# Splitting the state recurrence of an S4 layer's channel loop into two alternating vector chains

## The chip, the core and the metric

The kernel runs on one core of a Trainium2 chip. The metric is the device time of one execution in microseconds (us); lower is better. Before the change three runs took 2869.94, 2877.78 and 2879.02 us, so the median is 2877.78 us.

A core has a matrix engine (TensorE, "PE" in the profile, with its weight loads as "PEld"), a vector engine (VectorE, "DVE"), a scalar engine (ScalarE, "ACT"), a general engine (GpSimd, "POOL") and an engine that mostly issues transfers (SyncE, "SP"). Each has its own instruction queue and runs it in order. Engines wait for each other, and an instruction waits for an earlier one of its own engine, through semaphores that finished instructions raise.

## The reference, cut to what matters

The program computes a gated mix of two layers over 2048 tokens of width 576, and all gradients of it. One layer is multi-head attention (32 heads of 18), the other a diagonal state-space layer (S4) with 128 complex states per channel, written in the reference as a long convolution:

```python
def _fwd_reference(A_x, ..., B_Dskip, gate_w):
    x = A_x                                             # (1, 2048, 576)
    g = _sigmoid((x * gate_w).sum(-1, keepdims=True))
    a = _A_ref(x, A_wqkv, A_wo)                         # attention
    b = _B_ref(x, B_A_re, ..., B_Dskip)                 # S4
    return g * a + (1 - g) * b

def _B_ref(u, A_re, A_im, B_re, B_im, C_re, C_im, log_dt, Dskip):
    dt = jnp.exp(log_dt)[:, None]
    logdA = dt * (A_re + 1j * A_im)                     # (576, 128)
    dB = dt * (B_re + 1j * B_im)
    P = jnp.exp(logdA[:, :, None] * l[None, None, :])   # l = 0 .. 2047
    K = jnp.einsum("dn,dnl,dn->dl", Cc, P, dB).real
    ...                                                 # y = causal convolution of u with K, by FFT
    return y + u * Dskip[None, None, :]

def reference(...):
    _out, _vjp = jax.vjp(_f, A_x, ..., gate_w)
    return (_out, *_vjp(grad_out))                      # output and 12 gradients
```

The kernel does the convolution without an FFT. It cuts the 2048 tokens into 16 chunks of 128. Inside a chunk it multiplies by small Toeplitz matrices; from chunk to chunk it carries the 128 complex states of each channel, H(k) = UV(k) + Z * H(k-1), where Z is the state's factor over 128 tokens. The gradient needs the same recurrence once more, on the output gradient in reversed order (the adjoint states, G). Both recurrences use the same Z and do not depend on each other.

## The kernel before

The program has four stages in a row: projections and parameter preparation, the attention forward and backward pass (0.2 to 2.2 ms of the span), the channel loop of the S4 layer (from about 2.2 to 2.7 ms), and a final stage with the weight gradients and the outputs.

**The channel loop.** `for i in range(NBLK)` (line 1182) runs over 18 blocks of `CB` = 32 channels. The 128 states lie on the 128 partitions; channels and chunks lie along the free dimension. The order of the work on each engine is the order of the code (the stage is written under a manual schedule). In iteration `i` it is, for the computing engines:

- `k0(i+1)`, `uv(i+1, 0)`, `turn_e(i+1, 1)`: matrix products on TensorE, evacuated by ScalarE, that prepare the next block. `uv` produces `UV`, the input of the recurrence (bfloat16).
- `scan(i, 0, 15)` (lines 548 to 563): the two recurrences of block `i` on VectorE. The tile `HG` holds 4 rows (real and imaginary part `r`, times forward and adjoint `s`), 15 chunks and 32 channels in float32. A copy (line 553) fills chunk 0, then 14 steps of three instructions follow: a product with the real and the imaginary part of Z together (line 559, 256 elements per partition), the addition of `UV` (line 562, 128 elements) and the addition of the crossed half (line 563, 128 elements). Each of the three reads what the one in front of it wrote.
- `casts(i)` on ScalarE: bfloat16 copies `hR` and `gR` of the states (line 570).
- `rw1(i)` and `rw2(i)` on VectorE (lines 578, 584, 585): the states times parameters, which make `Rw`.
- `t0(i)`, `uv(i+1, 1)`, `ybp(i)`: TensorE products; `ybp` multiplies `Rw` (tile `yp`) and waits for it.
- `pairs1(i)` and `pairs2(i)`: products of states on VectorE (lines 629 and 657, tile `pq`), summed by TensorE into `misc`.
- `turn_e(i+2, 0)`, `m_sum`, `m_fin`, `sums(i)`, `m_part(i+3)`: further preparation on TensorE and ScalarE, and one short pair of instructions on GpSimd.

The loads of later blocks (`E1n`, `xs`, `T0w`, about 1 MB each) are issued by SyncE one to three iterations ahead. VectorE has nothing in the loop but `scan`, `rw1`, `rw2`, `pairs1` and `pairs2` of one block, then the same of the next. The final stage begins when the buffers of the loop come free, and its first weight gradients (`ps_dwq`) follow the last block's TensorE work.

The tile `tz` is a temporary of the recurrence with two buffers. `par` holds, for each block, Z as eight rows of 32 channels: four times the real part, then the imaginary part with the signs of the four rows.

Of the kernel before, what the change touches and what calls it, by code (L numbers as in the profile page):

```python
# [9 lines left out]
A = mybir.AluOpType  # L10
ACT = mybir.ActivationFunctionType
BF = mybir.dt.bfloat16
F32 = mybir.dt.float32
# [4 lines left out]
P = 128  # L18


def build(tc, aps, dbg_aps=None, stages=("s1", "attn", "post", "s4", "final")):
    nc = tc.nc
# [39 lines left out]
    with ExitStack() as gctx:  # L62
# [38 lines left out]
        CB = 32  # L101
# [329 lines left out]
        Q = {}  # L431
# [73 lines left out]
        def blk(b):  # L505
            if b not in BK:
                B_ = BK[b] = dict(E={}, En={})
            return BK[b]
# [39 lines left out]
        def scan(b, k0, k1):  # L548
            B_ = blk(b)
            UVk = B_["UV"][:, :, 0:2 * NB, :].rearrange("p r (s k) c -> p r s k c", s=2)  # L550
            if k0 == 0:
                B_["HG"] = Q["pw"].tile([P, 4, NS, CB], F32, tag="HG", name="HG")
                nc.vector.tensor_copy(B_["HG"][:, :, 0, :].rearrange("p (r s) c -> p r s c", s=2), UVk[:, :, :, 0, :])
                k0 = 1
            HG = B_["HG"]
            ZZ = B_["par"][:, 0:8, :].rearrange("p (m q) c -> p m q c", m=2)
            for k in range(k0, k1):
                tz = Q["pw"].tile([P, 2, 4, CB], F32, tag="tz", bufs=2, name="tz")
                nc.vector.tensor_tensor(tz, HG[:, :, k - 1, :].unsqueeze(1).to_broadcast([P, 2, 4, CB]), ZZ, op=A.mult)  # L559
                t0v = tz[:, 0].rearrange("p (r s) c -> p r s c", s=2)  # L560
                t1v = tz[:, 1].rearrange("p (r s) c -> p r s c", s=2)
                nc.vector.tensor_tensor(t0v, t0v, UVk[:, :, :, k, :], op=A.add)  # L562
                nc.vector.tensor_tensor(HG[:, :, k, :].rearrange("p (r s) c -> p r s c", s=2), t0v, t1v[:, ::-1], op=A.add)  # L563

        def casts(b):
            B_ = blk(b)
            HGv = B_["HG"].rearrange("p (r s) k c -> p r s k c", s=2)
            for nm, s_ in (("hR", 0), ("gR", 1)):
# [5 lines left out]
        def rw1(b):  # L574
            B_ = blk(b)
            for nm, r_, tg in (("wa", 8, "wA"), ("wb", 9, "wB")):
                B_[nm] = Q["pw"].tile([P, 4 * NS, CB], F32, tag=tg, name=nm)
                nc.vector.tensor_tensor(B_[nm], B_["HG"].rearrange("p q k c -> p (q k) c"),
                                        B_["par"][:, r_, :].unsqueeze(1).to_broadcast([P, 4 * NS, CB]), op=A.mult)
# [118 lines left out]
        if "attn" in stages:  # L698
# [5 lines left out]
            with ExitStack() as ctx:  # L704
# [293 lines left out]
                for G in range(NTOT + OFF + 24):  # L998
# [4 lines left out]
                    if G < NTOT:  # L1003
                        u, s = divmod(G, NST)
# [28 lines left out]
                    elif 0 <= m_ < NTOT // 8:  # L1033
# [14 lines left out]
                        else:  # L1048
                            p = 2 * kq + (slot == 4)
# [41 lines left out]
                    for (kind, g, b, i, j, ps) in rows:  # L1091
# [9 lines left out]
                        else:  # L1101
# [6 lines left out]
                            if U["dsn", i] == nj:  # L1108
                                p = i // 2
# [15 lines left out]
        if "s4" in stages:  # L1125
# [8 lines left out]
            with ExitStack() as ctx:  # L1134
                pc = ctx.enter_context(tc.tile_pool(name="s4l", reuse_waits="tile", bufs=1))
                pw = Q["pw"] = Q["en", 2] = ctx.enter_context(tc.tile_pool(name="s4lw", reuse_waits="tile", bufs=1))
# [45 lines left out]
                for i in range(NBLK):  # L1182
# [17 lines left out]
                    if cur:  # L1200
                        scan(i, 0, 15)
                        casts(i)
                        rw1(i)
                        rw2(i)
                        t0(i, 0)
                        t0(i, 1)
# [33 lines left out]
        if "final" in stages and "s4" in stages:  # L1240
# [14 lines left out]
            with ExitStack() as ctx:  # L1255
# [18 lines left out]
                with ExitStack() as actx:  # L1274
# [87 lines left out]
                    s_ = [SS[:, q, :] for q in range(6)]  # L1362
# [173 lines left out]
```

## Time and profile before

| what | value |
| --- | --- |
| runs | 2869.94, 2877.78, 2879.02 us; median 2877.78 us |
| the profiled execution's own time | 2882.82 us |
| span of its profile | 2881.1 us |
| mean granted TensorE clock | 0.924 |
| busy over the span | PE 86%, ACT 82%, DVE 82%, POOL 56% |
| channel loop, copies of line 553 of blocks 2 to 17 | 2272.4 to 2677.2 us, one every 26.9 to 27.3 us |
| the 14 steps of `scan` with the copy | 15.9 to 16.1 us per block from block 2 on |
| line 559, 252 times | 425 ns median |
| line 562 and line 563, 252 times each | 292 ns median each |

The profile is of one execution. Its times are in us from the start of the span unless marked ns. "Busy" is the time in which at least one instruction of an engine ran; instructions of one engine may overlap slightly, so that a start can lie before the end of the one in front. An entry such as "PE yp L30 <- DVE Rw L584: 27.1, 13" says that TensorE stood idle before an instruction that writes `yp` until VectorE's instruction of line 584 ended: 27.1 us in 13 cases. Many matrix instructions have line 30, since a helper records them; they are told apart by their tiles.

### The profile page before, as it was taken

What the parts mean: (1) busy time and instruction counts of PE and PEld (TensorE: products, weight loads), DVE (VectorE), ACT (ScalarE), POOL (GpSimd) and SP (SyncE); (2) the same over time, 40 slices, a digit from 0 to 9 for tenths busy, and PEclk for the clock granted to TensorE, in tenths of its full rate; (3) what the DMA queues carried; (4) which work ended last, traced back from release to release, by engine and by line L of the source; (5) the groups of instructions that cost most, each with busy time, mean ns of one, the idle gap of its engine ahead of it and who ended that gap; (6) DMA issues with size and microseconds to landing.
All of it is one profiled execution on the core that took longest, in us unless ns stands there. A gap on an engine that the chain in (4) does not pass through costs nothing.

```text
span 2881.1 us, 69609 instructions
## 1 busy us (share of the span) xinstructions
PE 2466.0 (86%) x27164; PEld 1180.8 (41%) x27164; DVE 2362.0 (82%) x4145; ACT 2374.7 (82%) x2792; POOL 1609.3 (56%) x2656
## 2 busy tenths in 40 slices
PE   4768889898888889898989989888986889888689
PEld 2332333233233233233333333333324788778457
DVE  4445999898888899888989989998975899999854
ACT  2449999999999999999999999999964777877121
POOL 1037888888888788888878878888511000000010
PEclk8886999999999999999999999999966888888799
DMA  8864989999998999997998998899798888885895
GB/s 222 167 165 91 158 158 172 157 161 165 165 161 158 170 160 160 167 169 151 168 169 153 164 173 157 157 173 156 142 162 205 234 220 224 230 216 156 235 235 138
DMA packets 1293510, 500.08 MB, mean 174 GB/s; under 512 B 1187813, under 2 KB 1263302, under 8 KB 1283962
## 3 DMA queue, kind: packets, MB, share of 16 engines
q1 hardware_dynamic: 1260474, 434.46, 79.1%
q0 software_dynamic: 20624, 53.26, 7.6%
q10 hardware_dynamic: 12080, 7.90, 1.0%
q8 instruction: 213, 3.49, 0.5%
q14 instruction: 119, 0.97, 0.1%
HBM read 144.56 MB, written 99.69 MB: 85 GB/s over the span
## 4 chain that ended last, share of the span: by engine, by line
ACT 36%; DVE 25%; PE 24%; DMA 7%; issue 6%; SPq 2%; POOL 0%; ACTq 0%; DVEq 0%; POOLq 0%
ACT eb L1100 21%; ACT PT L1095 13%; PE ps_P L30 7%; DVE ds L1105 7%; DVE tz L559 3%; DMA dsT<-ds 2%; PE accV L30 2%; DVE HG L563 2%; DVE tz L562 2%; PE ps_dx L30 2%; PE turn_p L843 2%; PE accK L30 2%; PE accO L30 1%; PE ps_dwq L30 1%; DVE pq L629 1%
## 5 line engine op out<-in xcount | busy, mean ns | idle before, releaser
L1105 DVE TENSOR_TENSOR ds<-ps_P,PT 128x512 bf16<-128x512 f32 x2048 | 1312.6, 683 | 138.3 <-PE ps_P L30 89.1
L1100 ACT ACTIVATE eb<-ps_P 128x1024 bf16<-128x1024 f32 x1024 | 1097.4, 1072 | 55.9 <-PE ps_P L30 55.6
L1095 ACT ACTIVATE PT<-ps_P 128x1024 bf16<-128x1024 f32 x1024 | 1100.6, 1077 | 14.4 <-PE ps_P L30 13.2
L30 PE MATMUL ps_P<-dOaT,VaT_g 32*128 32x512 bf16 x2048 | 584.9, 393 | 30.7 <-DVE ds L1105 15.0
L358 POOL TENSOR_TENSOR et<-eG,eT 128x448 f32<-128x448 f32 x576 | 542.0, 961 | 10.7
L30 PE MATMUL ps_P<-QaT_g,KaT_g 32*128 32x512 bf16 x2048 | 411.6, 395 | 137.3 <-ACT PT L1095 123.0
L30 PE MATMUL ps_P<-KaT_g,QaT_g 32*128 32x512 bf16 x2048 | 411.0, 394 | 1.8 <-ACT eb L1100 0.8
L30 PEld LDWEIGHTS <-KaT_g 32*128 32x128 bf16 x2048 | 147.7, 91 | 476.0 <-issue 461.6
L358 POOL TENSOR_TENSOR Eo<-et,et 128x448 bf16<-128x448 f32 x288 | 327.1, 1136 | 20.8
L665 POOL TENSOR_TENSOR SS<-m 128x96 f32<-128x96 f32 x18 | 10.0, 555 | 465.0 <-ACT m L663 465.0
L30 PEld LDWEIGHTS <-QaT_g 32*128 32x128 bf16 x2048 | 116.2, 91 | 290.7 <-issue 268.5
L30 PE MATMUL accO<-PT,Vtok_g 128*32 128x512 bf16 x2048 | 213.9, 404 | 0.0
L30 PE MATMUL accV<-eb,dOa 128*32 128x512 bf16 x2048 | 187.4, 399 | 27.3 <-ACT eb L1100 26.8
L30 PE MATMUL accK<-dsT,Qtok_g 128*32 128x256 bf16 x4096 | 165.4, 283 | 30.1 <-DMA dsT<-ds 28.1
L30 PE MATMUL accQ<-ds,Ktok_g 128*32 128x512 bf16 x2048 | 161.3, 393 | 2.1 <-DVE dvacc L897 2.0
L30 PEld LDWEIGHTS <-Vtok_g 128*32 128x32 bf16 x2048 | 53.7, 93 | 228.1 <-issue 227.3
L848 DVE COPY dsT<-turn_p 128x1024 bf16<-128x1024 bf16 (+1 forms) x216 | 139.3, 645 | 5.6 <-PE turn_p L843 5.6
L521 ACT COPY E1e<-etp 128x1024 bf16<-128x1024 bf16 x136 | 128.2, 1039 | 18.8 <-PE etp L520 18.4
L843 PE MATMUL turn_p<-ident_bf,ds 128*128 128x128 bf16 x1664 | 137.4, 226 | 1.6 <-DVE gb L915 0.8
L30 PEld LDWEIGHTS <-E1n 128*128 128x128 bf16 x2304 | 96.5, 108 | 87.4 <-issue 87.0
L30 PEld LDWEIGHTS <-Qtok_g 128*32 128x32 bf16 x4096 | 89.0, 97 | 95.0 <-issue 61.1
L30 PE MATMUL yp<-Rw,E1n 128*128 128x30 bf16 x1152 | 67.5, 232 | 64.8 <-DVE Rw L584 51.1
(251 smaller groups left out, 3730.8 us busy)
## 6 DMA issues: line engine op xcount, KB each, us to landing
E_d<-Eo POOLq DMA_DIRECT2D x144, 256.0 KB, 3.8
E1n<-E_d SPq DMA_DIRECT2D x36, 1024.0 KB
xs<-xb_d SPq DMA_DIRECT2D x18, 1024.0 KB
T0w<-Kp_d SPq DMA_DIRECT2D x18, 1024.0 KB
Md_d<-mst SPq DMA_DIRECT2D x36, 288.0 KB
dsT<-ds SPq DMA_TRANSPOSE x512
dqkv_d<-dtk POOLq DMA_DIRECT2D x96, 72.0 KB, 4.5
QKV_d<-stg SPq DMA_DIRECT2D x12, 504.0 KB
```

The source lines that it names most:

```text
L30: return nc.tensor.matmul(out, lhsT=lhsT, rhs=rhs, start=start, stop=stop, **kw)
L358: nc.gpsimd.tensor_tensor(out, a, b, op=op)
L521: copy(E_[:, 4 * q:4 * q + 4], pt_)
L559: nc.vector.tensor_tensor(tz, HG[:, :, k - 1, :].unsqueeze(1).to_broadcast([P, 2, 4, CB]), ZZ, op=A.mult)
L562: nc.vector.tensor_tensor(t0v, t0v, UVk[:, :, :, k, :], op=A.add)
L563: nc.vector.tensor_tensor(HG[:, :, k, :].rearrange("p (r s) c -> p r s c", s=2), t0v, t1v[:, ::-1], op=A.add)
L629: nc.vector.tensor_tensor(o.rearrange("p a b n c -> p a b (n c)"), a_.rearrange("p b n c -> p b (n c)").unsqueeze(1).to_broadcast([P, 2, 2 ...
L843: nc.tensor.transpose(pt_[:, x, qb, :], t_[:, qb * P:(qb + 1) * P], ident_bf)
L848: (nc.scalar.copy if NTOT <= now[0] < NTOT + OFF else nc.vector.tensor_copy)(o_(), pt_[:, x:x + n])
L1095: nc.scalar.activation(U["PT"][i, j // 2], ps, ACT.Exp)
L1100: nc.scalar.activation(e, ps, ACT.Exp)
L1105: nc.vector.tensor_tensor(U["ds"][i][:, j, :], ps, U["PT"][i, j // 2][:, j % 2, :], op=A.mult)
```

## The change

In `scan`, each step's three instructions over both recurrences become six: for each of product, addition of `UV` and addition of the crossed half, first the forward recurrence (`s_` = 0), then the adjoint (`s_` = 1), each half as wide. The temporary becomes two, `tz0` and `tz1`, each with two buffers of half the size. `HG` stays one tile; its views are only reordered. The rest of the program stays as it is.

```diff
-            HG = B_["HG"]
-            ZZ = B_["par"][:, 0:8, :].rearrange("p (m q) c -> p m q c", m=2)
+            HG = B_["HG"].rearrange("p (r s) k c -> p s r k c", s=2)
+            ZZ = B_["par"][:, 0:8, :].rearrange("p (m r s) c -> p s m r c", m=2, s=2)
             for k in range(k0, k1):
-                tz = Q["pw"].tile([P, 2, 4, CB], F32, tag="tz", bufs=2, name="tz")
-                nc.vector.tensor_tensor(tz, HG[:, :, k - 1, :].unsqueeze(1).to_broadcast([P, 2, 4, CB]), ZZ, op=A.mult)
-                t0v = tz[:, 0].rearrange("p (r s) c -> p r s c", s=2)
-                t1v = tz[:, 1].rearrange("p (r s) c -> p r s c", s=2)
-                nc.vector.tensor_tensor(t0v, t0v, UVk[:, :, :, k, :], op=A.add)
-                nc.vector.tensor_tensor(HG[:, :, k, :].rearrange("p (r s) c -> p r s c", s=2), t0v, t1v[:, ::-1], op=A.add)
+                tz = [Q["pw"].tile([P, 2, 2, CB], F32, tag=f"tz{s_}", bufs=2, name="tz") for s_ in range(2)]
+                for s_ in range(2):
+                    nc.vector.tensor_tensor(tz[s_], HG[:, s_, :, k - 1, :].unsqueeze(1).to_broadcast([P, 2, 2, CB]), ZZ[:, s_], op=A.mult)
+                for s_ in range(2):
+                    nc.vector.tensor_tensor(tz[s_][:, 0], tz[s_][:, 0], UVk[:, :, s_, k, :], op=A.add)
+                for s_ in range(2):
+                    nc.vector.tensor_tensor(HG[:, s_, :, k, :], tz[s_][:, 0], tz[s_][:, 1, ::-1], op=A.add)
```

So the 14 steps of a block hold 84 vector instructions in place of 42. The product has 128 elements per partition in place of 256, the additions 64 in place of 128. An instruction now needs the result of the second instruction in front of it, not of the one directly in front.

## The prediction

> **What bounds the kernel now.** The change touches one loop only, so the first view is the busy time of each engine by stretches of 27 us, about one iteration of the channel loop (us; PE, PEld, DVE, ACT, POOL busy, then granted clock, DMA share, GB/s).
>
> ```profile
> 2371.00:2398.00 27.00, 23.58 (x390) 22.38 (x389) 25.32 (x53) 21.13 (x33) 1.06 (x2) 0.87 0.83 202
> 2398.00:2425.00 27.00, 23.71 (x390) 22.49 (x389) 25.32 (x53) 21.21 (x33) 0.90 (x2) 0.81 0.86 239
> ```
>
> VectorE has the highest sum, 25.32 of 27, and the 1.68 that are missing are not waits for other engines: 43 dependent starts of a few hundredths each make nearly all of them. The second view, who waited for whom from 2240 to 2640 us (total, times, longest), agrees: VectorE's only entry above 1 us is a single 7.1 us at the start of that stretch, while TensorE waits for VectorE:
>
> ```profile
> PE yp L30 <- DVE Rw L584: 27.1, 13, 3.0
> PE yp L30 <- DVE Rw L585: 11.1, 13, 0.9
> DVE pq L629 <- ACT hR L570: 7.1, 1, 7.1
> ```
>
> Per block TensorE loses (27.1 + 11.1) / 13 = 2.94 us to it. Third, the chain that ended last is VectorE without a break from 2272 us (block 2) to 2699.9 us (end of block 17). So a block costs VectorE's length, 26.95 us from one copy of line 553 to the next. In blocks 0 and 1 the chain runs through ScalarE, TensorE and DMA; time won there is lost.
>
> Fourth, VectorE's timeline (start, us, instruction), the end of a block's recurrence:
>
> ```profile
> 2394.05 0.42 DVE L559 TENSOR_TENSOR tz<-HG,par 128x256 f32<-128x256 f32 x1
> 2394.51 0.29 DVE L562 TENSOR_TENSOR tz<-tz,UV 128x128 f32<-128x128 f32 x1
> 2394.83 0.29 DVE L563 TENSOR_TENSOR HG<-tz 128x128 f32<-128x128 f32 x1
> 2395.16 0.43 DVE L559 TENSOR_TENSOR tz<-HG,par 128x256 f32<-128x256 f32 x1
> ...
> 2398.41 2.15 DVE L578 TENSOR_TENSOR wb<-HG,par 128x1920 f32<-128x1920 f32 x1
> 2400.60 1.16 DVE L584 TENSOR_TENSOR Rw<-wb,wa 128x960 bf16<-128x960 f32 x1
> 2401.68 1.15 DVE L585 SCALAR_TENSOR_TENSOR Rw<-wa,wb 128x960 bf16<-128x960 f32 x1
> ```
>
> Line 562 begins 34 ns after line 559 ends (medians of the unrounded records, the same behind lines 562 and 563), because it reads what 559 wrote. Line 585 does not need line 584: it begins before 584 has ended, 2401.68 against 2400.60 + 1.16. Unrounded it is 82 ns before, and over all independent pairs 80 to 86 ns. A dependence thus costs 34 + 83 = 117 ns per instruction, and the recurrence pays it three times a step. The change puts an independent instruction between the two.
>
> **Widths.** One product of lone elements gives the fixed part:
>
> ```profile
> L1253 DVE TENSOR_TENSOR dsg<-sgo,ggo x16: 159/159/160, 2775.9 to 2857.0; 128x1 f32<-128x1 f32 x16
> L559 DVE TENSOR_TENSOR tz<-HG,par x252: 424/425/576, 2211.1 to 2692.2; 128x256 f32<-128x256 f32 x126
> L562 DVE TENSOR_TENSOR tz<-tz,UV x252: 291/292/482, 2211.5 to 2692.6; 128x128 f32<-128x128 f32 x126
> ```
>
> From 128 to 256 elements 133 ns are added, 1.04 ns each; from 1 to 128 again 133. So a width of 64 takes 159 + 63 x 1.04 = 225 ns. Halving 128 saves only 67 of 292.
>
> **The step before.** (425 + 34) + 2 x (292 + 34) = 1111 ns.
>
> **The step after.** Call the pairs A (product), B and C (additions), 0 forward and 1 adjoint. I take a start as the later of two times: 83 ns before the end of the instruction in front, and 34 ns after the end of the one it needs. A0 starts at 0 and ends at 292; A1 starts at 209 and ends at 501; B0 at 418 (its need allows 326); B1 at 418 + 225 - 83 = 560 (need: 535); C0 at 702 (677); C1 at 844 (819); the next A0 at 986 (961). The step is 2 x 209 + 4 x 142 = 986 ns, 125 less, and the tightest margin is 25 ns. The last step has nothing to overlap with: C1 ends at 844 + 225 = 1069 where line 563 ended at 1077. A block saves 13 x 125 + 8 = 1633 ns, 1.63 us.
>
> The unknown is the start of an instruction whose need was met just before. The trace has instructions that wait for VectorE's own semaphore and overlap all the same. In the final stage:
>
> ```profile
> 2716.90 0.76 DVE L1364 SCALAR_TENSOR_TENSOR SS<-fta,SS 128x576 f32<-128x576 f32 x1
> 2717.58 0.75 DVE L1253 TENSOR_TENSOR o_t<-zz,SS 128x576 f32<-128x576 f32 x1
> 2718.25 0.75 DVE L1253 TENSOR_TENSOR fta<-zz,SS 128x576 f32<-128x576 f32 x1
> ```
>
> The third overwrites `fta`, which line 1364 still reads, so its record carries a wait; it begins 83 ns before the second ends. But that wait had been met for 0.59 us; here it is met 59 ns before the start. With a delay L from an end to the start behind it, the step is 986 for L up to 59 and 866 + 2L above (A0 to B0 stays 418, the two others become 225 + L). It equals 1111 at L = 122. The dependent starts show L = 34, and I take that, as the nearest row; the other end, no overlap for any instruction that waits, is priced as a rival.
>
> A rule of the Trainium skill speaks against the change: "VectorE: DVE Perf Modes", section "The DRAIN you can't avoid", has the next operation start only once the pipe is empty, semaphore or not, and its "Rules for kernel authors" say to minimize the count of operations. By it a step would be 2 x 292 + 4 x 225 = 1484 ns even without gaps, and 16 blocks would lose 14 x 373 ns each, 84 us. The page itself limits the rule to operations that are held, and the rows above with starts 80 to 86 ns early are not; so I side with the trace.
>
> **What else moves.** `tz0` and `tz1` take the room of `tz`; no transfer, no wait on another engine and no queue changes. The first product still follows the copy of line 553 (34 ns), and its waits for `par` stay. VectorE fetches 42 more instructions a block; a price for that isn't shown: TensorE runs 390 instructions in the same time, so I take nothing, and up to 0.2 us a block as the other end, about what the records of each block have of slower instructions now (15.97 us for 0.25 + 14 x 1.11 = 15.8).
>
> **Who is next.** A block on VectorE becomes 26.95 - 1.63 = 25.3 us. TensorE needs 26.95 - 2.94 = 24.0, among it 0.76 of waiting for ScalarE's `wk`. ScalarE is busy for 21.2, and `hR`, which VectorE needs behind `Rw`, ends at 2426.35 for a need at 2429.9 in one block: 3.5 us of cover, 1.9 afterwards. DMA: 0.85 x 26.95 = 22.9 us of its engines' time, a share of 0.90; a stretch at 0.94 is shown. So VectorE stays last by 1.3 us, and all of 1.63 passes through. TensorE's denser work may lower its clock: in the two stretches above the clock differs by 0.06 and PE busy by 0.13 us, within the 1.3.
>
> The gain counts in blocks 2 to 17: 16 x 1.63 = 26.1 us. If it also came through in blocks 0 and 1 it would be 29.4. Behind the loop `ps_dwq` starts at 2708.0, directly behind the last `misc`, and its loads are issued from 2674.8 on as buffers of block 16 come free; they lose 1.6 us of lead, so at most 1.6 us can come back. The profiled execution's 2882.82 would become 2856.7. It lies 0.2% above the median; the same 26.1 off the median of 2877.78 gives 2851.7.
>
> **Rivals.**
> 1. The wait hides the overlap (slower). If an instruction with a wait on its own engine begins only after the end of the one in front, whether met or not, a step is 2 x 292 + 4 x 225 + 6 x 34 = 1688 ns: +577, times 14 x 16 = +129 us, 3007 us. Against it: the last fence above. For it: the wait there had been met for 0.59 us, ten times as long as here. It decides from L = 122 ns; at L = 150 the step is 1166, +12 us.
> 2. The halves are taken as dependent (no change). They interleave in one tile `HG`. If the next A0 is made to wait for C1, it starts at 1069 + 34 = 1103: 8 ns a step, 1.8 us in all, 2876 us. Against: in the attention stage VectorE's copies into `dsT` (line 848) write pieces that interleave with those that a transfer writes, and the view of that line names only TensorE as what it waited for.
> 3. Another resource takes over in the loop (a smaller gain). With TensorE, DMA or fetching at 26 us a block, 16 x 0.95 = 15 us remain, 2863. For it: the 1.3 us of cover is thin, TensorE already carries 24.0. Against: the waits for `Rw` in 13 of 13 blocks.
>
> **How the numbers follow.** Forecast (24 to 29 us saved) 0.70; rival 3, 0.11; rival 2, 0.08; rival 1, 0.11. A measurement of this kernel can tell about 0.3% (8.6 us). Faster: 0.70 + 0.11 = 0.81; within: 0.08; slower: 0.11. Predicted is the likeliest case, 2852 us. The range goes from all 18 blocks with 4 us of scatter, 2844, to 2868, which takes in rival 3 with the scatter and leaves out rivals 1 and 2, 0.19.
>
> **What would show it.** Right: lines 559, 562 and 563 with 504 instructions each at about 292, 225 and 225 ns, though VectorE's busy time hardly falls; starts of a step about 986 ns apart; 14.3 us for a block's recurrence with the copy; a block in 25.3 us; TensorE's wait for `Rw` shortened by about 1.6 us to 1.3. Wrong: steps above 1111 ns, or A0 34 ns behind C1 (rival 2), or steps of 986 with blocks that stay near 27 us and VectorE waiting for ScalarE or TensorE (rival 3).

## The result, and the profile after

Four runs of the changed kernel have a median of 2846.94 us (2837.63 to 2849.11); the kernel before stood at 2875.45 us beside them. The ratio is 0.9896, with a 95% interval of 0.9867 to 0.9925: the change makes the kernel 28.5 us faster. The prediction was 2852 us, with a range of 2844 to 2868. The profiled execution took 2849.11 us, its span is 2847.4 us.

The channel loop after, VectorE's timeline (start, us, instruction; "x2" stands for a forward and an adjoint instruction):

```profile
2406.73 0.35 DVE L562 TENSOR_TENSOR tz<-tz,UV 128x64 f32<-128x64 f32 x2
2407.00 0.35 DVE L564 TENSOR_TENSOR HG<-tz 128x64 f32<-128x64 f32 x2
2407.27 0.48 DVE L560 TENSOR_TENSOR tz<-HG,par 128x128 f32<-128x128 f32 x2
2407.67 0.35 DVE L562 TENSOR_TENSOR tz<-tz,UV 128x64 f32<-128x64 f32 x2
```

From one addition of `UV` to the next, 2406.73 to 2407.67, a step takes 0.94 us. It was 1.11. Every pair begins before the one in front has ended: 2406.73 + 0.35 is 2407.08, and line 564 is there at 2407.00. No start waits for a result. The unrounded records give a median step of 946 ns, with starts 202 ns apart behind a product and 135 or 136 behind an addition, each about 81 ns before the end in front.

The view of the tile `tz` (count; shortest, median, longest in ns):

```profile
L560 DVE TENSOR_TENSOR tz<-HG,par x504: 275/284/501, 2213.2 to 2661.3; 128x128 f32<-128x128 f32 x168
L562 DVE TENSOR_TENSOR tz<-tz,UV x504: 207/217/443, 2213.7 to 2661.6; 128x64 f32<-128x64 f32 x168
L564 DVE TENSOR_TENSOR HG<-tz x504: 207/216/431, 2213.9 to 2661.9; 128x64 f32<-128x64 f32 x168
```

The durations are 8 ns below the 292 and 225 that the prediction used. Though twice as many instructions run, VectorE's busy time over the span is 2350.9 us after 2362.0. Most of what was won lay between the instructions: over blocks 2 to 15 VectorE's time without any instruction falls from 23.9 to 3.9 us, its busy time from 354.0 to 346.0.

Two stretches as long as one block (us; PE, PEld, DVE, ACT, POOL busy, granted clock, DMA share, GB/s), and who waited for whom from 2240 to 2600 us (sum of the wait, how often, longest; us):

```profile
2375.00:2400.00 25.00, 22.68 (x390) 21.42 (x389) 24.72 (x96) 21.81 (x34) 0.92 (x2) 0.93 1.05 228
2400.00:2425.00 25.00, 21.45 (x390) 20.02 (x389) 24.72 (x96) 20.97 (x33) 0.74 (x2) 1.00 0.90 256
```

```profile
PE yp L30 <- DVE Rw L586: 10.0, 13, 0.9
PE yp L30 <- DVE Rw L585: 7.6, 7, 2.5
```

VectorE is now busy for 24.72 of 25.00 us, and TensorE's wait for `Rw` fell from 38.2 us (2240 to 2640 us before) to 10.0 + 7.6 = 17.6 (2240 to 2600 us after), with 13 blocks in each. The 15 blocks from 2 to 16 take 24.95 to 25.03 us each, 24.99 in the mean, after 26.99. So VectorE still holds the block, with less to spare than before: the chain of work that ended last runs through VectorE without a break from 2343.8 us on (2268 before), and in blocks 2 and 3 it still passes through TensorE and ScalarE, though these blocks take 25.0 us like the others.

Where the span's 33.7 us came from: blocks 2 to 16 give 404.8 - 374.9 = 29.9 us. What follows the last block's first copy is 199.4 us after 203.9, of which 2.0 is block 17's own recurrence and the rest the scatter of the final stage. Block 2 begins 0.7 us later.

### The profile page after: what moved, and what is told of

Read it like the earlier page. It is cut to its first block, busy times and chain, and to the rows that moved or that the text cites. A ratio compares the mean times of both kernels' runs of the same rounds, so it can differ in the third digit from the quotient of the medians.

```text
span 2847.4 us, 70374 instructions
## 1 busy us (share of the span) xinstructions
PE 2449.0 (86%) x27164; PEld 1168.3 (41%) x27164; DVE 2350.9 (83%) x4901; ACT 2374.3 (83%) x2792; POOL 1611.3 (57%) x2656
## 5 line engine op out<-in xcount | busy, mean ns | idle before, releaser
L358 POOL TENSOR_TENSOR Eo<-et,et 128x448 bf16<-128x448 f32 x288 | 327.2, 1136 | 20.8
L560 DVE TENSOR_TENSOR tz<-HG,par 128x128 f32<-128x128 f32 x504 | 124.3, 287 | 0.6
L358 POOL TENSOR_TENSOR et<-eT 128x32 f32<-128x32 f32 (+3 forms) x288 | 116.1, 423 | 11.4
```

The lines of the kernel that those rows point to most:

```text
L358: nc.gpsimd.tensor_tensor(out, a, b, op=op)
L560: nc.vector.tensor_tensor(tz[s_], HG[:, s_, :, k - 1, :].unsqueeze(1).to_broadcast([P, 2, 2, CB]), ZZ[:, s_], op=A.mult)
```

## The experiments

**The order alone.** The same six half-wide instructions, one chain after the other:

```diff
                 for s_ in range(2):
                     nc.vector.tensor_tensor(tz[s_], HG[:, s_, :, k - 1, :]..., ZZ[:, s_], op=A.mult)
-                for s_ in range(2):
                     nc.vector.tensor_tensor(tz[s_][:, 0], tz[s_][:, 0], UVk[:, :, s_, k, :], op=A.add)
-                for s_ in range(2):
                     nc.vector.tensor_tensor(HG[:, s_, :, k, :], tz[s_][:, 0], tz[s_][:, 1, ::-1], op=A.add)
```

> The changed kernel's six half-wide instructions, but in the order product, addition, addition of the forward chain and then the same three of the adjoint chain, so that four of the six need the one directly in front. Theory (a dependence on the instruction directly in front costs 34 ns of waiting and 82 ns of lost overlap; the order is what the change brings): products start 82 ns before the end in front, additions 34 ns after it; a step is 2 x (318 + 259 + 143) = 1440 ns, a block of the loop 25.0 + 14 x 0.494 = 31.9 us, the whole 74 to 85 us above the kernel before, about 2955 us. Rival (narrower instructions alone bring the gain): steps of 946 ns, 2847 us.

Measured: 2957.89 us, ratio to before 1.0261 (1.0232 to 1.0289). VectorE's timeline in it:

```profile
2412.17 0.28 DVE L560 TENSOR_TENSOR tz<-HG,par 128x128 f32<-128x128 f32 x1
2412.49 0.22 DVE L561 TENSOR_TENSOR tz<-tz,UV 128x64 f32<-128x64 f32 x1
2412.74 0.22 DVE L562 TENSOR_TENSOR HG<-tz 128x64 f32<-128x64 f32 x1
2412.89 0.28 DVE L560 TENSOR_TENSOR tz<-HG,par 128x128 f32<-128x128 f32 x1
```

Within a chain, each addition begins behind the end in front (319 and 259 ns apart in the median); the next chain's product begins 143 ns after the last addition, before that has ended. A step is 2 x (319 + 259 + 143) = 1442 ns, 1440 expected, and a block takes 31.8 us. That is 6.8 us more than in the changed kernel, and the recurrence alone grows by as much, from 14.0 to 20.8 us. With the same instructions as the changed kernel, only the order turns 28 us won into 81 us lost.

**Extra instructions in the gaps.** The kernel before, with a filler behind each instruction of a step:

```diff
+            jk = Q["pw"].tile([P, 3, CB], F32, tag="jk", bufs=2, name="jk")
...
+                nc.vector.tensor_tensor(jk[:, 0], B_["par"][:, 0, :], B_["par"][:, 4, :], op=A.mult)   # and jk[:, 1], jk[:, 2]
```

> The kernel before, with one independent product of 32 elements per partition (its result is read by nobody) behind each of the three instructions of a step: 42 instructions more per block. Theory (the time between dependent instructions is idle and takes in another instruction for nothing): the fillers start 82 ns before the end of the instruction in front, the dependent ones still 34 ns after the end of what they need, the step stays at 1095 to 1115 ns, the time within 0.3% of before. Rival (every instruction costs its issue, about 102 ns at this width): 42 x 0.10 = 4.3 us a block, 69 us in all, about 2944 us.

Measured: 2882.51 us, ratio 1.0018 (0.9998 to 1.0038). VectorE's timeline (lines 561 and 565 are fillers):

```profile
2404.20 0.43 DVE L560 TENSOR_TENSOR tz<-HG,par 128x256 f32<-128x256 f32 x1
2404.54 0.18 DVE L561 TENSOR_TENSOR jk<-par 128x32 f32<-128x32 f32 x1
2404.66 0.29 DVE L564 TENSOR_TENSOR tz<-tz,UV 128x128 f32<-128x128 f32 x1
2404.87 0.18 DVE L565 TENSOR_TENSOR jk<-par 128x32 f32<-128x32 f32 x1
```

The filler of line 561 begins before the product has ended (2404.54 against 2404.63), and the addition is there 0.46 us after the product began, as without it. The median step is 1111 ns, 1112 without the fillers. 42 more instructions lengthen a block from 26.99 to 27.16 us, 4 ns for each, where 102 ns each was the rival's estimate. The count of instructions was not the cost; a dependence on the instruction directly in front was.

**Each part by itself.** Only the products split, and only the additions split:

```diff
-                nc.vector.tensor_tensor(tz, HG[:, :, k - 1, :].unsqueeze(1).to_broadcast([P, 2, 4, CB]), ZZ, op=A.mult)
+                for s_ in range(2):
+                    nc.vector.tensor_tensor(tzs[:, s_], ...[:, s_, :, k - 1, :].unsqueeze(1).to_broadcast([P, 2, 2, CB]), ...[:, s_], op=A.mult)
```

> The kernel before, with only the product split in two; the additions stay whole, so the first addition needs the second product directly in front of it. Theory: product 0 at 0, product 1 at 210, additions at 528 and 854, the next product at 1180 ns: 69 more than 1111, 16 x 14 x 0.069 = 15 us slower than before, about 2891 us. Rival (each part of the change brings its share): about 10 us faster than before.

```diff
-                nc.vector.tensor_tensor(t0v, t0v, UVk[:, :, :, k, :], op=A.add)
-                nc.vector.tensor_tensor(HG[:, :, k, :].rearrange(...), t0v, t1v[:, ::-1], op=A.add)
+                for s_ in range(2):
+                    nc.vector.tensor_tensor(t0v[:, :, s_], t0v[:, :, s_], UVk[:, :, s_, k, :], op=A.add)
+                for s_ in range(2):
+                    nc.vector.tensor_tensor(HG[:, :, k, :].rearrange(...)[:, :, s_], t0v[:, :, s_], t1v[:, ::-1, s_], op=A.add)
```

> The kernel before, with only the additions split in two and alternated; the product stays whole and needs the second addition directly in front of it. Theory: product at 0, the four additions at 459, 602, 737 and 872, the next product at 1123 ns: 12 more than 1111, 3 us in all, no difference that can be measured. Rival (each part of the change brings its share): about 18 us faster than before.

Measured: products alone 2895.48 us, ratio 1.0057 (1.0036 to 1.0079), step 209 + 319 + 326 + 326 = 1180 ns as expected; additions alone 2884.31 us, ratio 1.0026 (1.0010 to 1.0042), step 459 + 143 + 135 + 135 + 250 = 1122 ns, 1123 expected. Both are slightly slower than before (27.98 and 27.26 us a block for 26.99) and together they are faster: as long as one instruction per step needs the one in front, the narrow halves cost their fixed part and little is hidden.

**Other halves.** The two chains are channels 0 to 15 and 16 to 31:

```diff
+                cs = [slice(0, CH), slice(CH, CB)]
...
+                    nc.vector.tensor_tensor(tz[s_], HG[:, :, k - 1, cs[s_]].unsqueeze(1).to_broadcast([P, 2, 4, CH]), ZZ[:, :, :, cs[s_]], op=A.mult)
```

> The changed kernel, but the two alternating chains are the two halves of the 32 channels, each with both recurrences, in place of forward and adjoint. Theory (any two independent halves will do): the same steps of 946 ns and the same time within 0.3%, about 2847 us. Rival (runs of 16 elements in place of 32 cost more, or the halves within rows are taken as dependent): steps above 1000 ns, 12 us or more above the changed kernel.

Measured: 2849.92 us, ratio 0.9881 (0.9832 to 0.9929), blocks of 25.01 us in the mean. The median step is 946 ns again. Which halves alternate makes no difference.

**A need that is met late.** Chains of 8 channels:

```diff
+            for gk in range(4 * (k1 - k0)):
+                g_, k = divmod(gk, k1 - k0)
...
+                cs = slice(g_ * CG, (g_ + 1) * CG)     # CG = CB // 4, in every operand
```

> The changed kernel, but the two chains run over 8 channels at a time, four times one after the other: products of 32 and additions of 16 elements per partition, so short that an instruction's need is met after the engine could start it. Theory (a delay of 34 ns from the end of what is needed to the start, whatever lies between): starts 34 ns after the end of the second instruction in front, about 210, 193 and 193 ns from product to addition to addition to product of one chain, a step of 596 ns for 8 channels, 33 us a block for the recurrence, 45 us a block, 330 to 370 us slower than the changed kernel. Rival (a wait that is met only just before costs more when another instruction runs in between): more than 34 ns, up to the 52 that the changed kernel has to spare, 650 ns a step, or above.

Measured: 3250.7 us in one run, blocks of 47.8 us. The view of the tile `tz`:

```profile
L564 DVE TENSOR_TENSOR tz<-HG,par x2016: 177/191/445, 2218.8 to 3066.3; 128x32 f32<-128x32 f32 x184
L566 DVE TENSOR_TENSOR tz<-tz,UV x2016: 160/174/422, 2219.0 to 3066.5; 128x16 f32<-128x16 f32 x184
```

From the end of the second instruction in front to the start, the medians over some 2000 cases each are 34, 34 and 35 ns for addition, addition and product. So the delay does not grow because another instruction runs in between: that part of the theory holds. The step is 643 ns in the median, not 596, because the durations are 191 and 174 where the expectation took 176 and 159. 191 + 34, 174 + 34 and 174 + 35 make 642.

**What is next.** The changed kernel without the addition of `UV`:

```diff
-                for s_ in range(2):
-                    nc.vector.tensor_tensor(tz[s_][:, 0], tz[s_][:, 0], UVk[:, :, s_, k, :], op=A.add)
```

> The changed kernel without the addition of UV in the recurrence (28 instructions less a block; the states are then not those of the reference). VectorE's own work falls from 25.0 to 21.2 us a block. Theory (TensorE is next): blocks of 23.6 to 24.0 us, VectorE waits 2 us or more a block for the other engines, 16 to 22 us below the changed kernel, about 2828 us. Rival (nothing else is near): blocks of 21.3 us, 60 us below it, about 2787 us.

Measured: 2863.54 us, ratio to before 0.9942 (0.9919 to 0.9965): with less work on VectorE it is slower than the changed kernel, by 13 us going by the two ratios, by 16 us going by the blocks of the two profiles. Neither theory nor rival foresaw that. The blocks alternate, from 22.5 to 33.8 us (23.9 in the median, 26.07 in the mean), and the view of who waited for whom, from 2240 to 2620 us, says why (sum of the wait, how often, longest; us):

```profile
DVE pq L628 <- ACT hR L569: 74.7, 14, 13.1
ACT RX L453 <- DMA RXn<-gyr_d: 34.2, 7, 9.4
```

Every second block ScalarE stands before its copy of `RXn`, behind it in its queue `hR` comes late, and VectorE waits for `hR`. `RXn` is late because SyncE issues it late: the order of SyncE's queue in the loop is not fixed by the order of the code (the manual schedule of the loop names the other engines, not SyncE), and it differs from kernel to kernel though the loads in the code are the same. In the kernel before, the two halves of `RXn` (lines 442 and 443) stood so (SyncE's timeline):

```profile
2486.59 0.56 SPq L442 DMA_DIRECT2D RXn<-xr_d  x1
2487.25 1.89 SPq L530 DMA_DIRECT2D E1n<-E_d  x1
...
2489.98 5.08 SPq L530 DMA_DIRECT2D E1n<-E_d  x1
2495.22 1.32 SPq L477 DMA_DIRECT2D Md_d<-mst  x2
2496.60 0.71 SPq L443 DMA_DIRECT2D RXn<-gyr_d  x1
```

In the changed kernel both are issued ahead of `E1n`, 20 us before the copy that reads them (it starts at 2394.41):

```profile
2374.49 0.57 SPq L442 DMA_DIRECT2D RXn<-xr_d  x1
2375.11 2.93 SPq L443 DMA_DIRECT2D RXn<-gyr_d  x1
2378.14 1.15 SPq L530 DMA_DIRECT2D E1n<-E_d  x1
```

In the kernel without the addition they stand behind `Md_d` and `skw`, issued at 2449.48 for a copy that could have begun at 2451.6.

**Less work on VectorE that keeps the result.** `rw1` writes bfloat16, and one parameter row is stored with the other sign:

```diff
-                B_[nm] = Q["pw"].tile([P, 4 * NS, CB], F32, tag=tg, name=nm)
+                B_[nm] = Q["pw"].tile([P, 4 * NS, CB], BF, tag=tg, name=nm)
...
-            nc.vector.tensor_tensor(Rw[:, 0], wb[:, 2 * NS:], wa[:, 0:2 * NS], op=A.subtract)
-            nc.vector.scalar_tensor_tensor(Rw[:, 1], wa[:, 2 * NS:], -1.0, wb[:, 0:2 * NS], op0=A.mult, op1=A.subtract)
+            nc.vector.tensor_tensor(Rw[:, 0], wb[:, 2 * NS:], wa[:, 0:2 * NS], op=A.add)
+            nc.vector.tensor_tensor(Rw[:, 1], wa[:, 2 * NS:], wb[:, 0:2 * NS], op=A.subtract)
```

> The changed kernel, and the two products of rw1 written in bfloat16, one parameter row stored with the other sign, so that both halves of Rw are a plain sum or difference of bfloat16 operands. Theory (VectorE is still last by about 1 us a block): the two instructions that write Rw go from 1.08 to about 0.57 us from start to start, a block from 25.0 to 24.0 us, 16 us below the changed kernel, about 2831 us. Rival (another resource already holds the block at 25 us): less than 5 us below it.

Measured: 2845.21 us, ratio 0.9868 (0.9817 to 0.9919); not told apart from the changed kernel. `Rw` became as short as expected, in the view of that tile (shortest, median, longest in ns):

```profile
L585 DVE TENSOR_TENSOR Rw<-wb,wa x18: 657/658/728, 2231.3 to 2663.5; 128x960 bf16<-128x960 bf16 x18
```

Who waited for whom in this kernel, from 2240 to 2620 us:

```profile
DVE pq L630 <- ACT hR L571: 17.6, 6, 9.5
ACT RX L453 <- DMA RXn<-gyr_d: 5.5, 3, 2.4
```

Ten of the blocks take about 23.98 us, 1.0 less, but five of the 15 take 24.2 to 26.7, and block 1 grows from 34.3 to 38.2. The time is what the rival forecast, but not for its reason: in ten blocks nothing else holds VectorE at 25 us. In four of the five longer ones VectorE waits for `hR`, 0.8 to 2.8 us, after ScalarE has waited for `RXn` (two blocks) or for `par` (two). So late loads take back most of what VectorE gives.

**RXn earlier, and SyncE's order by hand.** First `RXn` alone, traced half an iteration earlier:

```diff
-                    if sb is not None and sb % 2 == 0:
-                        load_rx(sb // 2)
+                    if i == 0:
+                        load_rx(1)
...
                         prep_rx(sb)
+                        if sb % 2 == 1 and sb + 1 < NBLK:
+                            load_rx((sb + 1) // 2)
```

> The kernel with the bfloat16 products of rw1, and the load of RXn for the next pair of blocks traced one half iteration earlier, right behind the last copy that reads the buffer, so that both its halves are issued ahead of the stores of Md_d that wait for ScalarE. Theory (ScalarE waits for RXn only because SyncE issues it late, and VectorE then for hR): ScalarE's wait for RXn is gone, every block takes 24.0 us, about 15 us below the changed kernel, 2832 us. Rival (the DMA engines' rate holds the block): blocks stay at a mean of 24.5 us with another load named, 2845 us as without the move.

Measured: 2844.59 us, ratio 0.9888 (0.9857 to 0.9920). In the profile ScalarE's wait for `RXn` is gone and 14 of the 15 blocks take 23.95 to 24.02 us; one takes 28.7, with another load late, `par`, as the view of who waited for whom from 2400 to 2560 us has it:

```profile
DVE pq L630 <- ACT hR L571: 4.8, 1, 4.8
ACT wk L592 <- DMA par<-par_d: 4.2, 1, 4.2
```

The profiled execution was the fastest of the four, 2835.89 us; the other three took 2844 to 2845, and what held those no profile shows. The named wait was the right one, the forecast of 2832 us was not met.

Then SyncE's queue in the order of the code, with the loads placed by hand, for three kernels (the load of `RXn` stands where the last experiment put it):

```diff
+                ctx.enter_context(tc.manual_schedule(engines={mybir.EngineType.SP}))
                 for i in range(NBLK):
...
+                    if i == 0:
+                        load_rx(1)
+                    if mb is not None and i > 0:
+                        m_load(mb)
                     if sb is not None and i > 0:
                         m_skw(sb)
-                    if sb is not None:
-                        load_par(sb)
-                    if mb is not None:
-                        m_load(mb)
-                    if sb is not None and sb % 2 == 0:
-                        load_rx(sb // 2)
...
                         rw2(i)
+                        if sb is not None:
+                            load_par(sb)
```

> The kernel with the bfloat16 products of rw1, and SyncE's order of issue in the channel loop fixed by hand: xs, gyp, skw, the store of K0c, par behind rw2, RXn behind the copies that free its buffer, T0w, yd, E1n twice, the stores of Md_d. Theory: as with RXn moved alone, blocks of 24.0 us, 2832 us. Rival (any order leaves the DMA engines behind): blocks above 24.4 us, 2842 us or more.

> The changed kernel without the addition of UV (states not those of the reference, VectorE's own work 21.2 us a block), with the same order of SyncE by hand. Theory (with the load out of the way TensorE is next): even and odd blocks alike, 23.4 to 24.0 us, VectorE waiting 2 us or more a block for hR or misc, 16 to 24 us below the changed kernel, about 2827 us. Rival (the loads hold it): unequal blocks of 26 us in the mean as before the move, 2863 us.

> The changed kernel with the same order of SyncE by hand and nothing else. Theory (VectorE holds the block there, and no load is late): blocks of 25.0 us, 2847 us within 0.3%. Rival (the order of the loads was part of the change's gain): blocks away from 25.0 us and a difference of more than 9 us.

Measured: with the bfloat16 products 2853.21 us, ratio 0.9920 (0.9891 to 0.9950); without the addition of `UV` 2853.58, 0.9919 (0.9893 to 0.9945); the changed kernel 2861.30, 0.9933 (0.9912 to 0.9954). All three theories failed; the blocks are unequal, 25.99, 25.68 and 25.89 us in the mean. The last of the three is the telling one: the vector work is that of the changed kernel, only SyncE's order differs, and a third to a half of the gain is gone. The two ratios to the kernel before, 0.9933 and 0.9896, are 11 us apart, with intervals that overlap at their ends; the 15 blocks of the profiles, 25.89 us for 24.99, make 13 us. Its even blocks take 24.97 us, its odd ones 25.9 to 29.7. Who waited for whom, from 2240 to 2620 us:

```profile
ACT m L664 <- PE misc L30: 26.4, 7, 4.3
PE misc L30 <- DMA skw<-Md_d: 22.9, 12, 4.0
DVE pq L630 <- ACT hR L571: 21.6, 7, 9.0
```

Here `skw`, put behind `xs` and `gyp`, is what comes late: in the seven odd blocks from 3 to 15 TensorE's `misc` waits for it, ScalarE's `m` for `misc`, and behind `m` in ScalarE's queue `hR` comes late for VectorE. The DMA engines' share over blocks 2 to 15 is 0.88, in the changed kernel 0.91; that speaks for the order and against the rate of the DMA engines, though a rate that runs short for a few us at a time isn't excluded. So the gain of the change rests on VectorE being last, and that holds only while SyncE's order brings every load in time. None of these versions is clearly faster than the changed kernel.

## Why the prediction was right

The direction, the place and the mechanism were as forecast, and the time lies in the range. That the time came so near is in part luck: the gain of a step was forecast too small, what slow instructions take back of it was left out, and SyncE's new order did no harm. By its steps:

- **VectorE holds the block**: right. From block 2 on the saving of a block appears whole in the time, as far as the runs can tell: 16 blocks of 2.0 us are 32 us, and the interval of the ratio goes from 22 to 38 us.
- **A dependence on the instruction in front costs 117 ns, and alternation removes it**: right, and shown in both directions. Putting the same instructions in chain order brings the cost back; filling the gaps of the kernel before costs 4 ns an instruction.
- **L = 34 ns**: right. In the changed kernel no need is met so late that it shows, and where it is, with 8 channels, the delay is 34 to 35 ns. The working for larger L has a slip: the step is 868 + 2L, and from L = 126 on the first addition waits too, so L = 150 would give 1192 ns and 18 us, not 1166 and 12.
- **The step of 986 ns**: mis-sized by 40. An instruction that begins before the end in front is about 8 ns shorter than one that had to wait, 284 and 217 for 292 and 225; it overlaps by 81 ns, not 83. From start to start that is 202 and 135 ns for 209 and 142, about 7 ns six times. The rows were in the profile of before: of the products in the final stage with 576 elements, those that begin early take 751 ns in the median, those that wait 757.
- **1.63 us a block**: 2.00 measured. Of the larger step gain (1112 to 946 in the medians) a part is lost again, since the mean step fell only from 1127 to 979 ns. The slow instructions cost more than the 0.2 us the prediction left unchanged: in each block from 2 on two instructions of the recurrence take clearly longer than the others, in both kernels, and all 32 of them in each profile run at a time when GpSimd runs its pair on `SS`. No other instruction of the recurrence is more than 15 ns above its median. In the kernel before they take 1.2 to 1.7 times the median, 0.19 us a block in all; in the changed kernel, where the instructions are shorter, 1.7 to 2.0 times, 0.41 us a block. The timelines of VectorE and then of GpSimd in the changed kernel, in one block:

```profile
2405.35 0.78 DVE L562 TENSOR_TENSOR tz<-tz,UV 128x64 f32<-128x64 f32 x2
```

```profile
2405.30 0.40 POOL L666 TENSOR_TENSOR SS<-m 128x96 f32<-128x96 f32 x1 [24.40 <-ACT m L664]
2405.66 0.39 POOL L667 TENSOR_TENSOR SS<-m 128x96 f32<-128x96 f32 x1
```

- **No queue changes**: wrong, without harm here. SyncE's order of issue was set anew; it happened to put `RXn` earlier, which was luck. The hand-made order shows that another can cost 11 to 13 us.
- **TensorE is next at 24.0 us, 1.3 us below VectorE**: TensorE's wait for `Rw` fell to 1.35 us a block, as forecast, and its granted clock did not fall, as the prediction had feared: it is 0.92 over blocks 2 to 15, after 0.87. But the cover was named for the wrong engines. What comes up about 1 us below VectorE is a load (`RXn`, `skw`, `par`, as the order has it), through ScalarE's queue or TensorE's. The prediction had looked at the DMA engines' share, forecast at 0.90 and measured at 0.91 (the highest stretch shown for the loop before is 0.93, not 0.94), and not at when each load is issued. Where no load was late, blocks of 22.5 to 24.0 us were seen (the shortest of them behind long ones), so a limit of TensorE and ScalarE near that value may stand; it wasn't separated.
- **The rivals**: "the wait hides the overlap" and "halves taken as dependent" are excluded by the starts, 81 ns ahead of the end in front. "Another resource takes over" did not happen in blocks of 25 us. With VectorE's work reduced to 24 us it happened in the blocks in which a load came late, and not in the others.
- **The rule of the Trainium skill** ("VectorE: DVE Perf Modes", section "The DRAIN you can't avoid", and its "Rules for kernel authors"): the runs are against its advice for this case. Twice as many instructions took 166 ns less per step, because none of them had to start behind the end of the one in front.

## What to carry to other kernels

In a chain of short vector instructions, compare each start with the end in front: a start after the end, at every step, is a price that independent work in between removes; here it is 34 ns of waiting and 82 of lost overlap. In this loop splitting paid only when all instructions of the cycle were split and alternated; one that still needed its neighbour took the gain away, and pieces of 8 channels made a block 47.8 us long. When an engine that holds a loop gets faster, look at when each load of the loop is issued and needed, not only at the share of the DMA engines, and compare the issue order of the two kernels where the code doesn't fix it.

## What the runs showed of the hardware that was not expected

- A VectorE instruction that starts as early as it can is 8 ns shorter than one that waited (217 and 225 ns at 64 elements; 214, with an overlap of 78 ns in place of 81, when the halves are channels); one that waited while another was still running has the full duration (174 ns at 16 elements, where 159 + 15 x 1.04 is 175).
- The delay from the end of a needed instruction to the start is 34 to 35 ns, with or without an instruction running in between.
- Two VectorE instructions of the recurrence take 1.7 to 2.0 times their median while GpSimd runs its two short instructions on `SS` (409 to 427 ns for 217 at 64 elements in blocks 2 and 3 of the changed kernel). This was so in each of the 16 blocks looked at; which of their operands is the cause isn't shown.
